# Filler matmuls of an attention stage held at their step, and up to seven of them from the fourth step on

## The chip, the cores and the metric

One core of one Trainium2 chip runs the whole kernel. The metric is device time in microseconds (us), the median of the runs of one kernel on one chip; lower is better. The engines are named as in the profile: PE (matmuls; PEld its weight loads), DVE, ACT, POOL, and SP, which issues the DMAs.

## The reference, cut to what matters

Three parts follow each other on tensors of 4 batches, 576 tokens and 512 columns, all float32.

```
scores = q @ k.T / 8                      # 4 batches, 8 heads, 576 x 576, head size 64
scores = where(scores >= max(scores) - tau, scores, -1e9)
x = softmax(scores) @ v                   # heads joined: 4 x 576 x 512
u = x + (x.T @ U @ V).T                   # mix over the tokens, rank 32
x = u + relu(u @ w_ch1) @ w_ch2           # 512 -> 2048 -> 512
e = routed expert of each token           # 8 experts, by w_gate and a local gate
out = p[e] * (relu(x @ w1[e]) @ w2[e])    # 512 -> 1024 -> 512
```

## The kernel before, in words

Batch 0's attention runs alone (`attention_alone`, line 546): this is the first stage. After it, the attention of batch b runs interleaved with the dense layers (`channel`) of batch b-1, and the experts come last.

The first stage takes 4 pairs of heads, each in 5 row groups of 128 rows. A group has two tiles (the two heads, h = 0 and 1), the last of a pair one: 36 tiles. The name s0_1_3 is the scores of batch 0, pair 1, group 3. One step of the loop handles one tile and touches its neighbours:

- `mask` of the tile before (line 370, DVE), which is the last reader of that tile's scores;
- `scores` of the next tile (lines 320 and 322, PE: four matmuls, eight in group 4). The scores have two PSUM buffers (tag s), so scores of tile i+2 wait for the mask of tile i;
- `peak` (line 355, DVE, the row maximum), `exp` (line 366, ACT) and `limits` (line 359, DVE) of the tile;
- pieces of `back` of earlier groups: transposes of the probabilities (tp, line 423, PE) which ACT copies out (ptt, line 424), products with v (po, lines 442 to 446, PE), and the chain that adds the token mix (lines 468 to 515);
- last, `turn_over` (line 586): filler matmuls on a constant bf16 tile (idle, line 592), whose results nobody reads. Their number is what an estimate of the step's `back` work (`spent`) leaves of 0.8, in units of 0.2, so at most four (four more in step 0, and eight ahead of the loop).

The result tile of a step's fillers is taken in turn from the two PSUM buffers of the transposes (tag tp). So fillers wait for the ACT copy of the transposes that were in that buffer, and a transpose after them for the buffer after that.

A scheduler orders the instructions of each engine before the launch, by what it reckons to be ready; on the chip each engine takes them strictly in that order. `keep_in_program_order` ties an instruction behind the one written before it on its engine. It adds no wait. In the kernel before it holds the first filler of steps 0, 1 and 2 alone. The scheduler may put later fillers earlier, into steps of others.

Into the same stage fall the loads of q and k (raw, line 283; split into kh, kl and qs, lines 291 to 301), and the conversion of the dense weights (`convert`): loaded (cr, line 203), joined on ACT and DVE (lines 211 and 218), written to DRAM (wdram, line 242), and read back as wr (line 681), from which ACT makes w0h and w1h (line 688).

Of the kernel before, what the change touches and what calls it, by code (L numbers as in the profile page):

```python
# [103 lines left out]
def attention_channel_moe(ctx, tc, qk, vv, tau, umat, vrep, wch, wgl, wexp, consts, out):  # L104
# [43 lines left out]
    def bank(tag, shape, name):  # L148
        return BANKS["pool"].tile(shape, F32, tag=tag, name=name, bufs=BANKS["bufs"][tag])
# [370 lines left out]
    def link():  # L520

        while CHAIN:
            try:
                return next(CHAIN[0])
            except StopIteration:
                CHAIN.pop(0)
        return 0.0
# [32 lines left out]
    def attention_alone(b):  # L560

        pend, debt, loads = [], 0.0, []
        inps = {0: load_pair(b, 0)}
        seq = [(hp, g, h) for hp in range(NPAIR) for g in range(5) for h in range(1 if g == 4 else 2)]
        groups = {}

        def scores_of(i):
            hp, g, h = seq[i]
            if h == 0:
                groups[hp, g] = Group(b, hp, g, inps[hp])  # L570
            groups[hp, g].scores(h)

        def tile_of(i):
            if not 0 <= i < len(seq):
                return None, 0
            hp, g, h = seq[i]
            return groups[hp, g], h

        def piece():
            while pend:  # L580
                try:
                    return next(pend[0]) + link()
                except StopIteration:
                    pend.pop(0)
            return link()

        def turn_over(n, nm):

            if n > 0:
                t = bank("tp", [128, 512], f"idle{nm}")  # L590
                for j in range(n):
                    x = pe.matmul(t, lhsT=idle[:, :128], rhs=idle, start=True, stop=True)
                    if j == 0 and nm in (0, 1, 2):
                        tc.keep_in_program_order(x)

        turn_over(8, "a")
        scores_of(0)
        for i in range(len(seq) + 3):
            G, h = tile_of(i)
            P, ph = tile_of(i - 1)  # L600
            Q, qh = tile_of(i - 2)

            if P:
                P.mask(ph)
            if i + 1 < len(seq):
                scores_of(i + 1)
            if G:
                G.peak(h)
                G.exp(h)
                G.limits(h, h + 1)  # L610
            if G and h == 0 and G.key[2] == 1 and G.key[1] + 1 < NPAIR:
                inps[G.key[1] + 1] = load_pair(b, G.key[1] + 1, loads)
            if loads and next(loads[0], 1):
                loads.pop()
            if Q and Q.nh == 1:
                Q.norm()
            debt = max(debt + RATE, 0.0) if pend else 0.0
            spent = piece()
            debt -= spent
            while pend and debt > 0:  # L620
                c = piece()
                debt -= c
                spent += c
            turn_over(int((0.8 - spent) / 0.2) + (4 if i == 0 else 0), i)
            if Q and qh == Q.nh - 1:
                pend.append(back(*Q.key, Q.inp, Q))
            yield i
        while pend or CHAIN:
            piece()
# [236 lines left out]
    with tc.manual_schedule(engines={mybir.EngineType.Pool}):  # L866
        for i in attention_alone(0):
            if i >= 4:
                debt += 0.2 if i > 9 else 1
                while debt > 0:  # L870
                    next(conv, None)
                    debt -= 1
# [514 lines left out]
```

## Time and profile before

| | us |
|---|---|
| median of 3 runs | 1026.74 |
| the runs | 1026.74, 1026.70, 1029.19 |
| the profiled execution, whole | 1029.15 |
| its span | 1027.4 |
| PE busy | 993.8 |
| DVE busy | 718.8 |
| ACT busy | 610.8 |

All rows of the trace are from the one profiled execution; times in them count from the start of its span. A busy engine is one that has an instruction in flight: back-to-back matmuls overlap, so their durations do not add up to the time of a group. The granted clock is the share of TensorE's 2.4 GHz that the chip gave; 0.50 is 1.2 GHz.

### The profile page before, as it was taken

How to read it: one execution, taken by the hardware profiler on the slowest of the kernel's cores; microseconds unless marked ns; L12 is line 12 of the kernel's file. 1: busy time of each engine (PE TensorE's matmuls, PEld its weight loads, DVE VectorE, ACT ScalarE, POOL GpSimd, SP SyncE). 2: the span in 40 equal slices, each digit the busy share in tenths (PEclk: the TensorE clock that was granted, in tenths of full speed). 3: DMA queues.
4: the chain of work that ended last, by engine and by line, in shares of the span. 5: the costliest groups of instructions: out<-in, count | busy, mean ns of one | idle time of the engine just before them, and what ended most of it. 6: DMA issues, size and time to landing. Idle time of an engine off the chain costs nothing. (4 is left out here: it accounts for less than half of the span.)

```text
span 1027.4 us, 17797 instructions
## 1 busy us (share of the span) xinstructions
PE 993.8 (97%) x6309; PEld 831.8 (81%) x6309; DVE 718.8 (70%) x1771; ACT 610.8 (59%) x1242; POOL 157.9 (15%) x149
## 2 busy tenths in 40 slices
PE   8898899999999999999999999999999999999996
PEld 4666677778787787788888898999998798889884
DVE  7889787886778877877676564692469755566673
ACT  6787877776687777776565653432344344355562
POOL 3322145342000000000000000014400321120100
PEclk9999999999999999999999999999999999999998
DMA  7745487864323322423121110463154655566650
GB/s 216 240 126 168 144 265 241 281 204 150 114 97 92 123 80 77 125 95 89 56 68 42 42 45 28 140 212 127 39 196 151 201 178 185 174 193 198 194 184 16
DMA packets 58529, 143.72 MB, mean 140 GB/s; under 512 B 7421, under 2 KB 8573, under 8 KB 58432
## 3 DMA queue, kind: packets, MB, share of 16 engines
q1 hardware_dynamic: 55072, 132.27, 40.2%
q0 software_dynamic: 3360, 10.23, 3.0%
q8 instruction: 52, 0.85, 0.3%
q14 instruction: 45, 0.37, 0.1%
HBM read 124.65 MB, written 18.61 MB: 139 GB/s over the span
## 5 line engine op out<-in xcount | busy, mean ns | idle before, releaser
L1137 ACT ACTIVATE eh<-ew 128x512 fp32r<-128x512 f32 x160 | 94.0, 628 | 66.9 <-PE el L1253 51.8
L1138 DVE TENSOR_TENSOR el<-ew,eh 128x512 fp32r<-128x512 f32 x160 | 106.6, 692 | 37.4 <-ACT eh L1137 34.8
L370 DVE SCALAR_TENSOR_TENSOR p<-s,st,p 128x576 f32<-128x576 f32 x144 | 114.1, 814 | 18.5 <-ACT p L366 14.8
L710 PE MATMUL l<-uh,w0h 128*128 128x256 f32 (+2 forms) x352 | 126.7, 360 | 0.3 <-ACT yT L515 0.3
L366 ACT ACTIVATE p<-s,st 128x576 f32<-128x576 f32 x144 | 103.6, 739 | 34.9 <-DVE st L355 33.7
L711 PE MATMUL l<-ul,w0h 128*128 128x256 f32 (+2 forms) x352 | 122.6, 349 | 0.0
L712 PE MATMUL l<-uh,w0l 128*128 128x256 f32 (+2 forms) x352 | 122.3, 348 | 0.0
L355 DVE TENSOR_REDUCE st<-s 128x1 f32<-128x576 f32 x144 | 105.2, 749 | 16.2 <-PE s L322 15.2
L725 PE MATMUL l<-hh,w1h 128*128 128x512 f32 (+3 forms) x320 | 115.3, 360 | 0.0
L727 PE MATMUL l<-hh,w1l 128*128 128x512 f32 (+3 forms) x320 | 112.6, 352 | 0.0
L726 PE MATMUL l<-hl,w1h 128*128 128x512 f32 (+3 forms) x320 | 112.2, 351 | 0.0
L424 ACT ACTIVATE ptt<-tp 128x512 f32<-128x512 f32 (+1 forms) x192 | 88.6, 490 | 30.7 <-PE tp L423 30.5
L320 PE MATMUL s<-kh,qs 128*128 128x288 f32 x320 | 96.7, 321 | 7.1 <-DVE p L370 4.9
L689 POOL TENSOR_TENSOR w1l<-wr,w1h 128x512 fp32r<-128x512 f32 x24 | 32.4, 1359 | 457.9 <-DVE rha L995 426.2
L423 PE MATMUL tp<-cst,p 128*128 128x128 f32 x576 | 91.2, 276 | 2.6 <-ACT ptt L424 2.2
L730 DVE TENSOR_TENSOR yT<-l,yT 128x448 f32<-128x448 f32 (+2 forms) x96 | 50.0, 521 | 57.7 <-PE l L727 57.3
L322 PE MATMUL s<-kl,qs 128*128 128x288 f32 x320 | 89.6, 299 | 0.0
L380 ACT ACTIVATE p<-p,rv 128x576 f32<-128x576 f32 x108 | 78.6, 771 | 15.7 <-DVE rv L387 15.5
L423 PEld LDWEIGHTS tp<-cst,p 128*128 128x128 f32 x576 | 67.9, 140 | 19.2 <-ACT ptt L424 9.3
L320 PEld LDWEIGHTS s<-kh,qs 128*128 128x128 f32 x320 | 60.9, 190 | 17.1 <-DVE p L370 7.7
L443 PE MATMUL po<-ptt,v 128*64 128x256 f32 (+1 forms) x256 | 71.4, 416 | 2.2 <-ACT ptt L424 2.2
L442 PE MATMUL po<-ptt,v 128*64 128x256 f32 (+1 forms) x256 | 70.8, 416 | 1.3 <-ACT ptt L431 1.0
(610 smaller groups left out, 2441.1 us busy)
## 6 DMA issues: line engine op xcount, KB each, us to landing
ew<-in_wexp_dram SPq DMA_DIRECT2D x80, 512.0 KB, 4.5
wr<-wdram SPq DMA_DIRECT2D x128, 256.0 KB, 2.7
cr<-in_wch_dram SPq DMA_DIRECT2D x32, 512.0 KB, 5.4
raw<-in_qk_dram SPq DMA_DIRECT2D x30, 304.0 KB, 3.5
wdram<-w SPq DMA_DIRECT2D x32, 256.0 KB, 2.9
v<-in_vv_dram SPq DMA_DIRECT2D x16, 352.0 KB, 3.6
raw<-in_qk_dram SPq DMA_DIRECT2D x16, 320.0 KB, 3.1
raw<-in_qk_dram SPq DMA_DIRECT2D x16, 288.0 KB, 4.0
```

What stands on the lines that cost most here:

```text
L320: pe.matmul(s["t"][:, h, :288], lhsT=qs[:, qc:qc + 128], rhs=kh[:, k0:k0 + 288], start=(j == 0), stop=False)
L355: dve.tensor_reduce(out=self.st[:, 0, h:h + 1], in_=self.t[h], axis=AX.XY, op=ALU.max, negate=True)
L366: act.activation(self.halves(h), self.t[h], AF.Exp, bias=self.st[:, 0, h:h + 1])
L370: dve.scalar_tensor_tensor(out=p, in0=self.t[h], scalar=self.st[:, 1, h:h + 1], in1=p, op0=ALU.is_ge, op1=ALU.mult, accum_out=self.rvs[:, ...
L423: pe.transpose(tp[:, c - c0], src[:, c * 128:c * 128 + 128], ident)
L710: pe.matmul(pm, lhsT=w1h[:, wk], rhs=uh[k], start=(k == 0), stop=False)
L711: pe.matmul(pm, lhsT=w1h[:, wk], rhs=ul[k], start=False, stop=False)
L712: pe.matmul(pm, lhsT=w1l[:, wk], rhs=uh[k], start=False, stop=(k == 3))
L725: pe.matmul(pm, lhsT=w2h[:, wd], rhs=xh, start=(f == f0), stop=False)
L726: pe.matmul(pm, lhsT=w2h[:, wd], rhs=xl, start=False, stop=False)
L727: pe.matmul(pm, lhsT=w2l[:, wd], rhs=xh, start=False, stop=(f == f0 + 3))
L1138: dve.tensor_tensor(out=lo, in0=x, in1=hi.bitcast(F32), op=ALU.subtract)
```

## The change

```
         def turn_over(n, nm):
...
                     x = pe.matmul(t, lhsT=idle[:, :128], rhs=idle, start=True, stop=True)
-                    if j == 0 and nm in (0, 1, 2):
+                    if j == 0 and nm != "a":
                         tc.keep_in_program_order(x)
...
-            turn_over(int((0.8 - spent) / 0.2) + (4 if i == 0 else 0), i)
+            turn_over(int(((1.5 if i > 3 else 0.8) - spent) / 0.2) + (4 if i == 0 else 0), i)
```

The first filler of every step is tied behind the instruction written before it on PE. From step 4 on the number is what `spent` leaves of 1.5, at most seven. The program has 78 fillers in place of 35: 8, 8, 4, 4 and 4 ahead of step 4 in both, and then 50 in place of 7 (4 of step 5, and one each of steps 9, 18 and 27).

The scheduler's order of the other instructions in the first stage changes with it, on PE, DVE, ACT and SP; on POOL, and on all engines from some 30 instructions after the start of the dense layers on, it is the same. Three places follow.

PE, steps 3 to 5, before: tp0_0_0_0, _4 and _8 are the transposes of pair 0, group 0 in three buffers' turns, s0_0_2_1 and s0_0_3_0 the scores of group 2, h = 1, and of group 3, h = 0.

```order
L423 MATMUL tp0_0_0_0_247<-cst_62,p0_0_0_150 128x128 x4
L320 MATMUL s0_0_2_1_234<-kh0_98,qs0_97 128x288
L322 MATMUL s0_0_2_1_234<-kl0_99,qs0_97 128x288
L320 MATMUL s0_0_2_1_234<-kh0_98,qs0_97 128x288
L322 MATMUL s0_0_2_1_234<-kl0_99,qs0_97 128x288
L423 MATMUL tp0_0_0_4_253<-cst_62,p0_0_0_150 128x128 x4
L423 MATMUL tp0_0_0_8_259<-cst_62,p0_0_0_150 128x128
L320 MATMUL s0_0_3_0_267<-kh0_98,qs0_97 128x288
L322 MATMUL s0_0_3_0_267<-kl0_99,qs0_97 128x288
L320 MATMUL s0_0_3_0_267<-kh0_98,qs0_97 128x288
L322 MATMUL s0_0_3_0_267<-kl0_99,qs0_97 128x288
```

PE, the same place, after (the scores s0_0_2_1 now stand ahead of the first row):

```order
L423 MATMUL tp0_0_0_0_247<-cst_62,p0_0_0_150 128x128 x4
L423 MATMUL tp0_0_0_4_253<-cst_62,p0_0_0_150 128x128 x4
L423 MATMUL tp0_0_0_8_259<-cst_62,p0_0_0_150 128x128
L320 MATMUL s0_0_3_0_270<-kh0_98,qs0_97 128x288
L322 MATMUL s0_0_3_0_270<-kl0_99,qs0_97 128x288
L320 MATMUL s0_0_3_0_270<-kh0_98,qs0_97 128x288
L592 LDWEIGHTS idle_85
L592 MATMUL idle4_262<-idle_85 128x512
L592 LDWEIGHTS idle_85
L592 MATMUL idle4_262<-idle_85 128x512
L322 MATMUL s0_0_3_0_270<-kl0_99,qs0_97 128x288
```

The transposes moved behind the scores of group 2, and two fillers came between the third and the last matmul of s0_0_3_0; seven of step 5 follow.

ACT, the same steps, before: ptt is the copy of the transposes, p the exp, qs1 the load of pair 1's q out of raw1.

```order
L291 ACTIVATE kh1_202<-raw1_1_224 128x640
L424 ACTIVATE ptt0_0_0_246<-tp0_0_0_0_247 128x4x128
L366 ACTIVATE p0_0_2_214<-s0_0_2_0_216,st0_0_2_215 128x576
L299 ACTIVATE qs1_201<-raw1_2_242,t8_63 128x608
L424 ACTIVATE ptt0_0_0_246<-tp0_0_0_4_253 128x4x128
```

ACT, the same place, after:

```order
L291 ACTIVATE kh1_202<-raw1_1_224 128x640
L366 ACTIVATE p0_0_2_214<-s0_0_2_0_216,st0_0_2_215 128x576
L299 ACTIVATE qs1_201<-raw1_2_242,t8_63 128x608
L424 ACTIVATE ptt0_0_0_246<-tp0_0_0_0_247 128x4x128
L424 ACTIVATE ptt0_0_0_246<-tp0_0_0_4_253 128x4x128
```

The first copy moved behind qs1, which waits for a DMA.

ACT, pair 1, group 3, before: w0h is the first dense weight read back, yT the token mix of pair 0, p0_1_3 the two exps of group 3.

```order
L424 ACTIVATE ptt0_1_0_526<-tp0_1_1_0_594 128x4x128
L515 ACTIVATE yT0_363<-pu0_0_4_0_573 128x256
L688 ACTIVATE w0h0_0_1362<-wr0_0_0_1360 128x512
L515 ACTIVATE yT0_363<-pu0_0_4_256_578 128x320
L366 ACTIVATE p0_1_3_556<-s0_1_3_0_558,st0_1_3_557 128x576
L424 ACTIVATE ptt0_1_0_526<-tp0_1_1_4_600 128x4x128
L424 ACTIVATE ptt0_1_0_526<-tp0_1_1_8_606 128x128
L211 ACTIVATE top0_87<-cr0_1_512_443 128x512
L366 ACTIVATE p0_1_3_556<-s0_1_3_1_585,st0_1_3_557 128x576
```

ACT, the same place, after:

```order
L688 ACTIVATE w0h0_0_1422<-wr0_0_0_1420 128x512
L515 ACTIVATE yT0_371<-pu0_0_4_0_591 128x256
L366 ACTIVATE p0_1_3_574<-s0_1_3_0_576,st0_1_3_575 128x576
L515 ACTIVATE yT0_371<-pu0_0_4_256_596 128x320
L366 ACTIVATE p0_1_3_574<-s0_1_3_1_606,st0_1_3_575 128x576
L424 ACTIVATE ptt0_1_0_544<-tp0_1_1_0_615 128x4x128
L424 ACTIVATE ptt0_1_0_544<-tp0_1_1_4_621 128x4x128
L424 ACTIVATE ptt0_1_0_544<-tp0_1_1_8_627 128x128
```

The second exp moved ahead of all three copies; w0h, which waits for a DMA, still stands ahead of both exps.

## Rows read from the trace of the kernel before

**Rows 1.** Windows by stage: length, busy us of each engine (instructions), clock, DMA share, GB/s.

```profile
core 0: us, PE busy (x) PEld busy (x) DVE busy (x) ACT busy (x) POOL busy (x), PEclk, DMA share, GB/s
...
16.00:44.00 28.00, 24.52 (x171) 17.71 (x170) 26.88 (x66) 23.46 (x50) 9.31 (x8) 1.00 0.75 247
44.00:56.00 12.00, 10.15 (x59) 7.12 (x58) 8.46 (x21) 7.75 (x16) 5.46 (x4) 0.86 0.47 146
56.00:112.00 56.00, 48.74 (x368) 35.56 (x367) 50.24 (x122) 46.91 (x106) 10.30 (x8) 1.00 0.54 157
112.00:990.00 878.00, 870.04 (x5547) 743.39 (x5546) 605.47 (x1502) 509.76 (x1024) 121.60 (x112) 1.00 0.43 138
```

**Rows 2.** Windows of the weak stretch, columns as in Rows 1.

```profile
47.00:48.00 1.00, 0.00 (x0) 0.00 (x0) 0.03 (x1) 1.00 (x4) 0.87 (x1) 1.00 0.86 295
...
49.00:50.00 1.00, 1.00 (x6) 0.62 (x3) 0.05 (x1) 1.00 (x3) 0.00 (x0) 0.50 0.74 234
```

**Rows 3.** Waits of DVE from 16 to 112 us: total us, times, longest.

```profile
DVE p L370 <- ACT p L366: 3.3, 6, 1.0
DVE st L355 <- PE s L322: 2.6, 5, 0.9
DVE xsd L472 <- PE tx L468: 0.8, 2, 0.5
```

**Rows 4.** Timeline of PE: start, us, instruction, count; eight fillers in a row.

```profile
13.68 1.90 PE L592 MATMUL idle<-idle 128*128 128x512 bf16 x8
```

**Rows 5.** Timeline of PE, steps 4 and 5; idle us and releaser in brackets.

```profile
17.17 0.86 PE L423 MATMUL tp<-cst,p 128*128 128x128 f32 x5
19.24 0.40 PE L320 MATMUL s<-kh,qs 128*128 128x288 f32 x1 [1.20 <-DVE p L370]
19.48 0.30 PE L322 MATMUL s<-kl,qs 128*128 128x288 f32 x1
19.61 0.29 PE L320 MATMUL s<-kh,qs 128*128 128x288 f32 x1
```

**Rows 6.** Timeline of ACT, the same steps.

```profile
17.07 0.58 ACT L424 ACTIVATE ptt<-tp 128x512 f32<-128x512 f32 x1
...
18.74 0.80 ACT L299 ACTIVATE qs<-raw,t 128x608 fp32r<-128x608 f32 x1 [0.46 <-DMA raw<-in_qk_dram]
19.45 0.74 ACT L424 ACTIVATE ptt<-tp 128x512 f32<-128x512 f32 x2
```

**Rows 7.** Timeline of DVE, the same steps.

```profile
20.46 0.76 DVE L355 TENSOR_REDUCE st<-s 128x1 f32<-128x576 f32 x1
21.25 0.82 DVE L370 SCALAR_TENSOR_TENSOR p<-s,st,p 128x576 f32<-128x576 f32 x1
```

**Rows 8.** Timeline of ACT around the first dense weight.

```profile
46.43 0.63 ACT L688 ACTIVATE w0h<-wr 128x512 fp32r<-128x512 f32 x1 [0.84 <-DMA wr<-wdram]
...
47.28 0.73 ACT L366 ACTIVATE p<-s,st 128x576 f32<-128x576 f32 x1
47.90 0.76 ACT L424 ACTIVATE ptt<-tp 128x512 f32<-128x512 f32 x2
...
49.17 0.74 ACT L366 ACTIVATE p<-s,st 128x576 f32<-128x576 f32 x1
```

**Rows 9.** Timeline of PE, the same place.

```profile
48.55 0.46 PE L443 MATMUL po<-ptt,v 128*64 128x256 f32 x1 [1.85 <-ACT ptt L424]
```

**Rows 10.** Timeline of DVE, the same place.

```profile
48.05 0.82 DVE L370 SCALAR_TENSOR_TENSOR p<-s,st,p 128x576 f32<-128x576 f32 x1 [1.01 <-ACT p L366]
...
49.95 0.82 DVE L370 SCALAR_TENSOR_TENSOR p<-s,st,p 128x576 f32<-128x576 f32 x1 [0.95 <-ACT p L366]
...
51.71 0.76 DVE L355 TENSOR_REDUCE st<-s 128x1 f32<-128x576 f32 x1 [0.94 <-PE s L322]
```

**Rows 11.** Timeline of SP's DMA queue: the reads of the first dense weights.

```profile
41.03 0.90 SPq L681 DMA_DIRECT2D wr<-wdram  x2
```

**Rows 12.** Window of the transposes (tile tp) alone: PE, PEld, ACT, clock, DMA.

```profile
80.00:82.00 2.00, 0.79 (x8) 0.55 (x6) 0.62 (x2) 1.00 0.62 225
```

**Rows 13.** Timeline of PE: the first matmul of the dense layers.

```profile
114.42 0.50 PE L710 MATMUL l<-uh,w0h 128*128 128x512 f32 x1 [0.32 <-ACT yT L515]
```

More of the change, by code (lines that the diff above doesn't have):

```diff
@@ L592, in turn_over @@
                     x = pe.matmul(t, lhsT=idle[:, :128], rhs=idle, start=True, stop=True)
-                    if j == 0 and nm in (0, 1, 2):
+                    if j == 0 and nm != "a":
                         tc.keep_in_program_order(x)
@@ L623, in attention_alone @@
                 spent += c
-            turn_over(int((0.8 - spent) / 0.2) + (4 if i == 0 else 0), i)
+            turn_over(int(((1.5 if i > 3 else 0.8) - spent) / 0.2) + (4 if i == 0 else 0), i)
             if Q and qh == Q.nh - 1:
```

## The prediction

> **What bounds the kernel now.** I read the windows by stage first [rows 1]. From 112 to 990 us PE is busy for 870.04 of 878 us, at full clock: whatever the first stage gains or loses is passed on one to one, and a matmul that moves out of the long stretch into a gap of the first stage saves its own time. The change touches the first stage only, so everything is decided between 16 and 112 us. There PE is busy for 24.52 + 10.15 + 48.74 = 83.4 us of 96, idle for 12.6. DVE is the denser engine by far in what it has to do: 26.88 of 28 us up to 44, and 50.24 of 56 behind 56. So the stage is set by DVE and by what DVE waits for. These waits come next [rows 3]: masks wait 3.3 us for exps of ACT, peaks 2.6 us for scores of PE, and 0.8 us goes to the token mix. Only the last two, 3.4 us, name PE.
>
> Third, the weak stretch, 44 to 56 us, where DVE is busy for 8.46 of 12 us and the mean granted clock is 0.86 [rows 1]. The order of events: ACT stands for 0.84 us until the first dense weight has landed, and its next exp starts at 47.28 [rows 8]. PE has nothing for 1.85 us, until 48.55 [rows 9]. In 49 to 50 its clock is 0.50, 1.2 GHz [rows 2]. DVE loses 1.01 and 0.95 us on late exps and 0.94 us on late scores, 2.90 us together [rows 10]. This is the only fall of the clock between 16 and 112 us.
>
> **The change part by part.** *More fillers.* Eight in a row take 1.90 us at full clock [rows 4]; the last takes its full 0.38 us to end, so one costs (1.90 - 0.38) / 7 = 0.217 us. There are 43 more, 9.3 us of PE. Beside the 12.6 us that PE is idle this fits in the sum, with 3 us to spare; it does not show that each falls where PE is idle. The cover, worked out: when a mask frees a score buffer, DVE has a peak (0.76 us) and a mask (0.82 us [rows 7]) to do before it wants the next scores, 1.58 us. The four score matmuls start 0.13 us apart and the last takes 0.3 us to end [rows 5], 0.7 us. The remaining 0.88 us hold four fillers. So up to four are free if they start no later than the mask ends, and they cost their time where they start late. Groups of seven exist only in step 5, and there the next scores wait for a mask anyway.
>
> *Steps 4 and 5.* Here I can follow the new order with the old durations. The scores s0_0_3_0 start at 19.24 now, released by a mask, and their peak runs at 20.46 [rows 5, 7]. In the new order the ninth transpose ahead of them reuses the buffer of tp0_0_0_0, whose copy now stands behind qs1. That load starts at 18.74, when its DMA lands, so the copy runs at 19.45 (now it ran at 17.07) and ends at about 20.0 [rows 6]. Transpose and three score matmuls: 20.1 to 20.5. Then two fillers, which wait for the second copy (to 20.4): 20.5 to 20.95. The last score matmul ends at about 21.35. The peak is late by 21.35 - 20.46 = 0.9 us, on DVE, with nothing else queued that could run. PE meanwhile idles from about 18.1 to 20.0. The next scores wait for the mask behind this peak, so the seven fillers of step 5 are hidden. Cost 0.9 us; bounds 0.4 (if only the copy counts) and 1.4 (if the clock falls after that gap too, as it did after 1.85 us [rows 9], at half speed for the fillers and the scores).
>
> *The weak stretch.* No filler stands where the gap is: in the new order PE still waits for the mask of s0_1_3, that for the exp, that for w0h, and that for the DMA. SP issues the read at 41.03 [rows 11]; in the new order it stands behind the same kinds of loads, so I leave it there. The first exp stays at 47.28. What changes is behind it: the second exp comes right after one yT copy, at about 48.25 instead of 49.17 [rows 8], so its mask can follow the first at 48.9 instead of 49.95 and that wait of 0.95 us goes. The scores s0_1_4 get their buffer at 48.9; their second half stands behind a transpose that waits for the copy of tp0_1_1_0 (now behind both exps, to 49.5), two products and four matmuls: they end at 50.6 at full clock, 51.2 at half clock, against 51.71 for the peak now [rows 10]. Gain 0.5 to 1.1 us. I take 0.8.
>
> Here a rule of the Trainium skill bears on what the fillers are for. Rows first: between 56 and 112 us the clock is 1.00 throughout [rows 1], also in 80 to 82, where eight transposes keep PE busy for 0.79 of 2 us [rows 12]. The Trainium skill, "TensorE: Matmul & The Clock Gate", Part 4 (PE-mode transpose), says that transposes do not count as activity for the clock. By that rule a stage with so many transposes needs fillers, and the change would be worth more than I give it. The trace does not bear it out, so I leave it out of the sum.
>
> *The end of the stage.* The new order puts the first four matmuls of s1_0_2 ahead of the dense layers. Now these start at 114.42 after waiting for the last token mix on ACT [rows 13], and those four come later, in the stretch that PE bounds. That moves 4 x 0.13 = 0.5 us into a gap. It is lost again if PE reaches the dense layers late because of them, so the bounds are -0.5 and +0.3.
>
> *The rest.* Some 30 steps keep their work and get other neighbours on DVE and ACT. The masks come earlier against the peaks. With the waits outside the two places at 3.4 + 3.3 - 2.9 = 3.8 us at most, I bound this at -2 (half goes) and +2.5 (half as much again, and the fillers of five steps start one filler late), and take 0.
>
> Sum on the profiled execution: 1029.15 + 0.9 - 0.8 - 0.5 = 1028.75, so -0.4. That execution is one of two kinds: the runs are 1026.70, 1026.74 and 1029.19, and it lies with the slow one. If the fall of the clock is what tells them apart (the 0.94 us and what follows it), the median has less to gain. Against the median, 1026.74 - 0.4: **1026.4 us**.
>
> **The rivals.** *Faster: the stage is freed of PE's delays.* If the fillers keep PE ahead at every step, the 2.90 us of the weak stretch and the other 2.6 - 0.94 = 1.7 us of late scores go: 4.6 us, less what the median run does not have, 1022.2 to 1024; I take 1023.0. For it: the new order alternates peak and mask more evenly, and frees buffers sooner. Against it: only 3.4 us of the waits name PE, the weak stretch is begun by a DMA, and a filler never makes real work earlier.
>
> *Slower: pinned fillers block the scores.* Fillers take a transpose buffer, so each group waits for an ACT copy, and the scores written behind now wait with it on PE. Some ten groups of step 4 and later stand directly ahead of scores or inside a group of them (steps 4, 9, 10, 16, 18, 24, 25, 27, 28, 30). The price of one is the 0.9 us worked out for step 4; if half of them pay it, 4.5 us: 1031.2. It decides where the copy ends later than a mask plus 0.88 us less the fillers' own time, which for four fillers is: later than the mask. For it: ACT is busy for 46.91 of 56 us [rows 1] and its copies stand behind exps. Against it: an exp that delays the copy delays the mask as well.
>
> *The change does not do what it says.* The gap at 47 to 48 lies in a chain of waits, not at the place of a filler; the clock falls there as before, and in the new gap at 18 to 20 perhaps too. Then the time is 1026.4 to 1028.9, still no difference by the bound below.
>
> **How the numbers follow.** A measurement of this kernel tells a change of about 0.3%, 3.1 us, from none. The forecast, with the case that the clock still falls, has 0.58: within 1023.7 and 1029.8. Faster by more has 0.22, slower by more 0.20: the slow rival needs five of ten places, the fast one nearly all of the waits that it names. If all terms go one way their bounds add to 0.4 - 1.1 - 0.5 - 2 = -3.2 and to 1.4 - 0.5 + 0.3 + 2.5 = 3.7; the range reaches a little into both rivals: 1022.8 to 1030.4.
>
> **What would show it.** DVE should wait for about 0.9 us for the scores near 20 us that it does not wait for now, and PE idle for some 2 us ahead of it. The first exp after w0h should start at 47 to 48.5, and the second about 1 us behind it. 78 fillers, with the waits of PE on ptt copies in their rows; the three kinds of DVE's waits [rows 3] at 5 to 9 us together, against 6.7 now. The dense layers should start at 113 to 116. I am wrong if that start moves by more than 3 us, or if the long stretch behind it changes its length.

## The result: 1040.04 us, slower by 1.1%

The changed kernel takes 1040.04 us (median of 4 runs, 1037.62 to 1040.68) against 1027.24 us before (4 runs, 1026.70 to 1029.19). The ratio is 1.011, with a 95% interval of 1.0092 to 1.0128. I had forecast 1026.4 and no difference. The profiled execution took 1040.34 us, 11.2 us more than that of before (1029.15).

The windows by stage, columns as in [rows 1], now read:

```profile
core 0: us, PE busy (x) PEld busy (x) DVE busy (x) ACT busy (x) POOL busy (x), PEclk, DMA share, GB/s
16.00:44.00 28.00, 25.20 (x153) 17.25 (x157) 26.00 (x64) 21.58 (x42) 9.28 (x8) 1.00 0.71 226
44.00:56.00 12.00, 11.24 (x89) 8.22 (x88) 9.08 (x24) 10.47 (x23) 4.67 (x4) 1.00 0.53 170
56.00:112.00 56.00, 49.43 (x348) 36.12 (x353) 45.09 (x107) 43.44 (x94) 11.49 (x9) 1.00 0.48 140
112.00:990.00 878.00, 865.91 (x5531) 739.03 (x5531) 602.08 (x1502) 508.60 (x1024) 120.84 (x112) 1.00 0.41 136
```

The granted clock between 44 and 56 us is 1.00 where it was 0.86. But DVE, the denser engine of the stage, does less in the 56 us behind it: 45.09 us of work for 50.24. PE does hardly more (49.43 for 48.74), although it has fillers to do. So the fillers mostly did not fill idle time; real work moved out of the window. What DVE and PE wait for from 16 to 112 us (total us, times, longest; DVE's rows answer to [rows 3]):

```profile
DVE st L355 <- PE s L322: 9.4, 13, 1.2
DVE p L370 <- ACT p L366: 3.7, 6, 1.0
```

```profile
PE idle L592 <- ACT ptt L424: 2.9, 6, 1.1
PE tp L423 <- ACT ptt L424: 2.0, 5, 0.7
PE pu L514 <- DVE th L501: 1.9, 3, 1.2
PE tT L490 <- ACT xsd L482: 1.4, 2, 0.9
PE s L320 <- DVE st L359: 0.8, 1, 0.8
PE s L320 <- DVE p L370: 0.6, 2, 0.3
```

Peaks wait for scores of PE for 9.4 us where it was 2.6. PE in turn waits for ACT and DVE, and hardly for masks (0.6 us, before 4.3). PE has become the late one. The dense layers, [rows 13] before, start 7.43 us later:

```profile
121.85 0.50 PE L710 MATMUL l<-uh,w0h 128*128 128x512 f32 x1 [0.51 <-ACT yT L515]
```

Behind that start the shift still grows: the last matmul of line 710, near the end of the dense layers, starts at 756.3 us for 742.7, 13.6 us late. The experts behind it give 2.4 us back. One gap stands out near 136 us (timelines of PE, ACT and SP's queue, and the window behind it):

```profile
136.54 0.65 PE L443 MATMUL po<-ptt,v 128*64 128x256 f32 x2 [2.15 <-ACT ptt L424]
```

```profile
133.77 0.78 ACT L211 ACTIVATE top<-cr 128x512 f16<-128x512 bf16 x1 [2.16 <-DMA cr<-in_wch_dram]
```

```profile
127.65 1.79 SPq L203 DMA_DIRECT2D cr<-in_wch_dram  x1
```

```profile
136.00:142.00 6.00, 5.46 (x18) 4.08 (x19) 2.01 (x3) 1.55 (x4) 3.93 (x5) 0.72 0.67 239
```

ACT stands for 2.16 us for a load of the conversion of the dense weights, with the copy that PE needs behind it. PE is idle for 2.15 us, and the mean granted clock from 136 to 142 us is 0.72. In the kernel before the same issue of SP took 0.43 us, ACT stood for its load for 0.73 us, and PE for the copy for 0.32:

```profile
120.22 0.43 SPq L203 DMA_DIRECT2D cr<-in_wch_dram  x1
```

```profile
124.97 0.79 ACT L211 ACTIVATE top<-cr 128x512 f16<-128x512 bf16 x1 [0.73 <-DMA cr<-in_wch_dram]
```

```profile
127.74 0.65 PE L443 MATMUL po<-ptt,v 128*64 128x256 f32 x2 [0.32 <-ACT ptt L424]
```

### The profile page after: what moved, and what is told of

It is laid out like the page before. It is cut to its first block, busy times and chain, and to the rows that moved or that the text cites. A ratio compares the mean times of both kernels' runs of the same rounds, so it can differ in the third digit from the quotient of the medians.

```text
span 1038.6 us, 17859 instructions
## 1 busy us (share of the span) xinstructions
PE 1002.1 (96%) x6343; PEld 837.5 (81%) x6352; DVE 717.7 (69%) x1771; ACT 613.8 (59%) x1242; POOL 157.9 (15%) x149
## 5 line engine op out<-in xcount | busy, mean ns | idle before, releaser
L443 PE MATMUL po<-ptt,v 128*64 128x256 f32 (+1 forms) x256 | 71.3, 414 | 2.1 <-ACT ptt L424 2.1
L714 DVE SCALAR_TENSOR_TENSOR hl<-l,hh 128x512 fp32r<-128x512 f32 (+2 forms) x80 | 46.3, 579 | 38.6 <-ACT hh L713 38.3
```

## The experiments

The table has the ratio to the kernel before (on the same chip, in the same minutes), its 95% interval, and the start of the dense layers in the one profiled execution; before it is 114.42. The absolute times of a kernel differ from chip to chip (the kernel before had medians of 1028.15 to 1033.77 us), so ratios are compared, and starts as one execution each. Runs 1 to 4, 5 to 8, 9 to 11, 12 to 15, 16 and 17, and 18 shared a chip and its runs of before.

| run | order of the real work | fillers of step 4 and later | ratio | interval | dense start, us |
|---|---|---|---|---|---|
| changed kernel | new | 50 | 1.011 | 1.0092 to 1.0128 | 121.85 |
| 1 bare | new | 34, short | 1.0125 | 1.0090 to 1.0161 | 121.42 |
| 2 half | new | 50, half length | 1.0110 | 1.0081 to 1.0139 | 121.49 |
| 3 pin only | old but for 4 places | 7 | 0.9993 | 0.9977 to 1.0008 | 112.90 |
| 4 more only | between | 50 | 1.0087 | 1.0069 to 1.0105 | 121.32 |
| 5 old order | old | 50 | 1.0043 | 1.0020 to 1.0066 | 119.77 |
| 6 new order | new | 7 | 1.0072 | 1.0035 to 1.0109 | 123.69 |
| 7 first half | new to 68 us | 7 | 1.0057 | 1.0031 to 1.0083 | 118.48 |
| 8 second half | new from 68 us | 7 | 1.0087 | 1.0057 to 1.0118 | 118.74 |
| 9 old order, bare | old | 36, short | 1.0048 | 1.0030 to 1.0067 | 116.30 |
| 10 scores first | scores early | 50 | 1.0147 | 1.0113 to 1.0180 | 131.81 |
| 11 same, before | scores early | 7 | 1.0029 | 1.0014 to 1.0045 | 117.82 |
| 12 no turn | old | 50, no own bank | 1.0064 | 1.0045 to 1.0083 | 118.90 |
| 13 run 5 again | old | 50 | 1.0070 | 1.0057 to 1.0083 | 118.32 |
| 14 run 6 again | new | 7 | 1.0069 | 1.0057 to 1.0081 | 119.67 |
| 15 changed again | new | 50 | 1.0101 | 1.0086 to 1.0116 | 124.86 |
| 16 scores whole | new, 13 tiles mended | 50 | 1.0111 | 1.0080 to 1.0142 | 122.52 |
| 17 same, before | old, 9 tiles mended | 7 | 1.0019 | 1.0001 to 1.0036 | 118.38 |
| 18 spared | old | 38 | 1.0039 | 1.0023 to 1.0056 | 116.31 |

The starts carry less than the ratios. Two executions of one program differ in theirs by 1.5 us (runs 5 and 13), 3.0 (the changed kernel and run 15) and 4.0 (runs 6 and 14). The profiled executions of runs 13 and 14 took 2.4 and 2.5 us less than the median of their run, that of run 8 7.5 us less, that of run 17 4.0 us more.

A second table shows where time is lost: by how much the peak (line 355) of the last tile of each pair of heads starts later than in the profile of before, from DVE's timelines, then the dense layers and the last matmul of line 710, near their end. In runs 5 and 13 one record of a peak is missing; their later peaks are counted accordingly. Run 8 has the order of before up to the middle of pair 2. It and run 3 show that the execution of before had itself lost over a microsecond by the end of pair 1.

| | pair 0 | pair 1 | pair 2 | pair 3 | dense layers | last of line 710 |
|---|---|---|---|---|---|---|
| start before, us | 25.99 | 51.71 | 74.47 | 95.76 | 114.42 | 742.7 |
| 3 pin only | +0.66 | -1.23 | -1.47 | -1.52 | -1.52 | -0.4 |
| 8 second half | +0.52 | -1.35 | +1.93 | +4.07 | +4.32 | +5.2 |
| changed kernel | +0.91 | +0.94 | +3.52 | +7.24 | +7.43 | +13.6 |
| 15 changed again | +1.02 | +0.95 | +5.54 | +9.20 | +10.44 | +13.2 |
| 14 new order | +0.65 | +0.05 | +2.39 | +5.01 | +5.25 | +6.4 |
| 6 new order | +1.52 | +0.99 | +3.15 | +7.19 | +9.27 | +11.5 |
| 13 old order, 50 fillers | +1.05 | +0.13 | +2.22 | +3.36 | +3.90 | +6.6 |
| 5 old order, 50 fillers | +1.90 | +0.38 | +2.47 | +3.61 | +5.35 | +7.9 |
| 9 old order, short fillers | +0.57 | -0.12 | +0.51 | +0.47 | +1.88 | +4.0 |
| 18 spared | +1.44 | +0.07 | +0.88 | +1.29 | +1.89 | +5.9 |
| 16 scores whole | +1.24 | +1.11 | +4.41 | +7.71 | +8.10 | +13.6 |

**Which half of the change costs?** Runs 3 and 4 make one half each (edits against the changed kernel).

```
-            turn_over(int(((1.5 if i > 3 else 0.8) - spent) / 0.2) + (4 if i == 0 else 0), i)
+            turn_over(int((0.8 - spent) / 0.2) + (4 if i == 0 else 0), i)
```

> Only the first half of the change: the first filler of every step is held at its step, the number stays at what is left of 0.8 (35 fillers). The order of the real work differs from before in four places only, all near steps 4 and 5. Both theories: no difference, 1026 to 1029, the dense layers at 114 to 115. If holding alone costs, as my slow rival has it, up to 0.9 us for each of the held groups of step 4 and later.

```
-                    if j == 0 and nm != "a":
+                    if j == 0 and nm in (0, 1, 2):
```

> Only the second half: 78 fillers, held in steps 0 to 2 alone, so the scheduler may put the others earlier, where it takes PE to be idle; its order of the real work lies between before and after. Theory A: the same 10.8 us of PE; if they float into idle time they are free, 1027 to 1030, if not, as the changed kernel, 1036 to 1041. Theory B: as far as the order is that of the changed kernel, the same loss; the order differs in about half of the rows, so 1030 to 1040.

Holding alone, with 7 late fillers, is free: 0.9993. The number alone costs 0.87%, most of the whole. So the holding, on which my slow rival rested, is not needed for the loss; whether it adds something to 50 fillers is open, since the intervals of run 4 and of the changed kernel overlap. Run 3 also has the clock at 1.00 in the weak stretch, with no filler there:

```profile
44.00:56.00 12.00, 10.31 (x68) 7.21 (x65) 9.99 (x27) 10.08 (x23) 5.45 (x4) 1.00 0.58 172
```

The order is not what keeps it up either. Run 8 (below) follows the kernel before in this stretch and has 1.00 too. ACT does not stand for the dense weight there, and PE's gap is 0.90 us in place of 1.85 (window, ACT, PE, and the two peaks at the ends of the stretch):

```profile
44.00:56.00 12.00, 10.31 (x67) 7.11 (x65) 10.01 (x27) 10.09 (x23) 5.46 (x4) 1.00 0.57 173
```

```profile
46.09 0.62 ACT L688 ACTIVATE w0h<-wr 128x512 fp32r<-128x512 f32 x1
```

```profile
48.21 0.43 PE L443 MATMUL po<-ptt,v 128*64 128x256 f32 x1 [0.90 <-ACT ptt L424]
```

```profile
46.89 0.75 DVE L355 TENSOR_REDUCE st<-s 128x1 f32<-128x576 f32 x1
...
51.89 0.76 DVE L355 TENSOR_REDUCE st<-s 128x1 f32<-128x576 f32 x1 [0.19 <-PE s L322]
```

The same two peaks before, and in the changed kernel:

```profile
46.28 0.75 DVE L355 TENSOR_REDUCE st<-s 128x1 f32<-128x576 f32 x1
...
53.86 0.73 DVE L355 TENSOR_REDUCE st<-s 128x1 f32<-128x576 f32 x1
```

```profile
48.47 0.76 DVE L355 TENSOR_REDUCE st<-s 128x1 f32<-128x576 f32 x1
...
54.96 0.75 DVE L355 TENSOR_REDUCE st<-s 128x1 f32<-128x576 f32 x1
```

The stretch takes 7.58 us before, 5.00 in run 8 and 6.49 in the changed kernel. Of the three profiles with the order of before in this stretch (before, runs 3 and 8), only that of before has the wait for the weight and the fall of the clock.

**Is it the fillers' own time?** In runs 1 and 2 the program is built as the changed kernel, and the filler instructions are then altered in place, so that nothing else moves. In run 1 those that carry a wait or a signal are cut to 32 columns and the others taken out; in run 2 all of step 4 and later are cut to 256.

```
+    drop(nc, lambda i: i > 3, 32)
```

> Every instruction stands in the order of the changed kernel; in the built program 16 of the 50 fillers of step 4 and later are taken out and the other 34, which carry a wait or a signal, are cut from 512 columns to 32. Theory A (the fillers' own PE time stands ahead of the scores): 50 x 0.217 = 10.8 us of PE go, of which 34 short ones keep perhaps 2; the waits of DVE for scores fall from 9.5 us to about 3, the dense layers start at 114 to 116 us in place of 121.85, and the time is 1027 to 1032. Theory B (the changed order of the real work, with the waits on the two transpose buffers, costs the time): the waits for scores stay at 8 to 10 us, the dense layers start at 120 to 122, the time is 1037 to 1041. If the clock falls again near 47 us for want of fillers, 1 to 2 us more in either. If the second loss (4 us between 122 and 240 us) comes with the order at the boundary, it stays under A too: 1031 to 1036.

```
+    shorten(nc, lambda i: i > 3, 256)
```

> The order of the changed kernel; the 50 fillers of step 4 and later are cut from 512 to 256 columns in the built program. Theory A (fillers' time): they take half, 5.4 us of 10.8; the dense layers start at 117 to 119 us, halfway between 114.4 and 121.85. Theory B (order and buffer waits): 120 to 122, and 1037 to 1041 in all.

Theory A, that the fillers' own time costs, is out as the main cause in the changed kernel: with nearly all of that time gone, the dense layers start only 0.43 us earlier and the ratio is 1.0125. Between the ends of pairs 1 and 3 run 1 still loses 5.2 us, where the changed kernel loses 6.3. The late scores stay (DVE's waits in run 1, 16 to 112 us):

```profile
DVE st L355 <- PE s L322: 8.3, 13, 1.1
DVE p L370 <- ACT p L366: 3.1, 4, 0.9
```

What the fillers do is to change the order: the scheduler reckons with their time when it draws up the order of everything else.

**The order and the fillers apart.** Edges that add no wait put the instructions of PE, DVE, ACT and SP of one kernel into the order of the other. (With its own order put in by such edges, the kernel before comes out instruction for instruction, so the edges cost nothing.) Run 5 has the fillers' number and the old order; run 6 the new order and the old number.

```
+        for a, b in zip(order, order[1:]):
+            tc.add_manual_dep(own[b], own[a].name, mybir.DependencyInfo(
+                mybir.DependencyClass.NoSync, mybir.DependencyReason.DATA), reason="follow")
```

> 78 full fillers, at nearly the places that they have in the changed kernel (7 behind the second score of step 5's tile, groups of 1 to 4 after), but every other instruction of PE, DVE, ACT and SP in the order of the kernel before; that order is imposed by edges that add no wait. Theory B (the scheduler's new order of the real work costs the time, the fillers' 0.217 us each are free): the dense layers start at 113 to 116 us, the time is 1026 to 1030. Theory A' (the fillers cost time by standing ahead of scores, whatever the order): 120 to 122 us and 1036 to 1041. The clock between 44 and 56 us should be 1.00 if the fillers keep it up.

> The kernel before, with its 35 fillers, and every other instruction of PE, DVE, ACT and SP in the order of the changed kernel. So none of the 50 later fillers is there, and none of their waits for an ACT copy of transposes. Theory B (order): the dense layers start at 120 to 122 us, the time is 1035 to 1041. The rival within it, that the fillers' waits for the transposes' buffers cost the time (my slow rival; the run with short fillers kept those waits): 114 to 117 us, 1027 to 1032.

Both cost. Runs 13 to 15 put these two and the changed kernel on one chip:

> The run with 78 fillers in the old order once more, beside the other three on one chip, for the share of the fillers' waits and turns. If order and waits add up to the whole: 1.003 to 1.006 here, 1.005 to 1.008 for the new order, 1.009 to 1.012 for the changed kernel. If either alone is enough: 1.008 to 1.012 in all three.

> The run with the new order and the 35 fillers of before once more, on the same chip. If order and waits add up: 1.005 to 1.008. If the order alone makes the whole loss: as the changed kernel, 1.009 to 1.012.

> The changed kernel itself, on the same chip and with a second profile. Ratio 1.009 to 1.013. If the gap of PE near 134 to 137 us and the fall of the clock behind it belong to this order, they are in this profile too, and the shift grows from 7 us at the dense start to 11 or more at 240 us; if they were chance, the shift stays at 7 to 10 us.

The new order alone costs 0.69%, the fillers alone 0.70%, both together 1.01%. Either alone makes two thirds of the loss, and they do not add up. I had expected them either to add up or to be enough alone; it is neither. (The same two programs on another chip gave 0.72% for the order, run 6, and 0.43% for the fillers, run 5.) In the new order alone peaks wait 7.5 us for scores (run 14; run 6 10.0), nearly as in the changed kernel; before it was 2.6:

```profile
DVE st L355 <- PE s L322: 7.5, 11, 1.1
```

So the order is enough for the late scores. What the fillers add to it, 0.3% between runs 14 and 15, does not go with their length in run 1, whose interval starts at 1.0090 (on another chip). Whether it is their waits for the two banks was not tested in the new order. Run 15 also settles that the gap near 136 us belongs to the changed kernel, since it is there again, 3 us later with the rest. The fall of the clock behind it is not there again (1.00 from 139 to 145 us):

```profile
139.56 0.65 PE L443 MATMUL po<-ptt,v 128*64 128x256 f32 x2 [2.16 <-ACT ptt L424]
```

In run 14, with the same order but the stage 5 us earlier, the wait there is 0.86 us:

```profile
133.07 0.65 PE L443 MATMUL po<-ptt,v 128*64 128x256 f32 x2 [0.86 <-ACT ptt L424]
```

**Which stretch of the order?** Runs 7 and 8 change over from one order to the other in the middle of pair 2.

```
+FOLLOW = {e: new[e][:cut[e]] + old[e][cut[e]:] for e in new}
```

> The kernel before with the changed kernel's order up to the middle of the third pair of heads (about 68 us: PE as far as the second scores of group 2) and its own order from there on. If the late scores are spread evenly, about half of the 7.4 us: the dense layers start at 117 to 119 us. If the loss is made where the first pair's steps 4 and 5 are, 119 to 122. The second loss behind the first stage (4 to 6 us) stays away if it comes from the order at the boundary: 1029 to 1032 in all; it is there if it comes from being late: 1032 to 1036.

> The reverse: the order of the kernel before up to the middle of the third pair, the changed kernel's from there on. Evenly spread late scores: the dense layers start at 117 to 119 us. If the second loss comes from the order at the boundary it is here: 1033 to 1038 in all; if not, 1029 to 1032.

The start moves by 4.1 and 4.3 us, near half each, as an even spread has it; with an execution of run 8 so far below its median this is a hint only. The ratios say no more than that each costs: 1.0057 and 1.0087 have intervals that overlap, and the second loss could not be read from them.

**Why do the fillers cost in the old order?** Three runs keep the old order. Run 9 cuts the fillers short as in run 1. In run 12 they take no bank of their own but are written into the tile of the next transposes, so that the waits and turns of the two banks go.

```
+    drop(nc, lambda i: i > 3, 32)
```

> The run with 78 fillers in the old order, whose dense layers started at 119.8 us, but in the built program 14 of the 50 later fillers are taken out and the other 36, which carry a wait or a signal, are cut to 32 columns. If in the old order the fillers cost by their own time, the start returns to 114 to 116 us and the time to that of before. If they cost by their waits for the transposes' buffers, and by the turn that they take of the two buffers, the start stays at 118 to 120 us.

```
                 tp = bank("tp", [128, 4, 128], f"tp{nm}_{c0}")
+                for _ in range(min(DUE[0], 4)):
+                    x = pe.matmul(tp.rearrange("p a b -> p (a b)"), lhsT=idle[:, :128], rhs=idle, start=True, stop=True)
```

> 78 full fillers and the order of the kernel before for all other work, as in the run with the old order, but the 50 later fillers take no bank of their own: they are written into the tile of the next transposes, just ahead of these, so they add no wait for an ACT copy that the transposes don't have anyway and no turn of the two banks. If the fillers' waits and turns cost the 0.4 to 0.5% that the old order with fillers showed, the time is that of before, ratio 0.998 to 1.002, the dense layers at 113 to 116 us. If the fillers' own 10.8 us of PE cost it, the ratio is 1.003 to 1.007 and the start 117 to 121 us.

Run 12 is against my rival: without own waits and turns the cost is still 0.64%. Run 9 is for the fillers' time inside the stage: the last peaks of its pairs follow those of before to within 0.6 us up to 96 us, where run 13 loses 3.4. So here, other than in the new order, the length of the fillers matters. A reason shows in windows of 8 us. The kernel before:

```profile
64.00:72.00 8.00, 7.84 (x66) 5.94 (x65) 6.71 (x20) 6.50 (x15) 1.27 (x1) 1.00 0.47 152
72.00:80.00 8.00, 7.95 (x59) 6.14 (x59) 7.44 (x20) 7.43 (x15) 2.93 (x2) 1.00 0.59 151
...
88.00:96.00 8.00, 7.59 (x71) 6.47 (x71) 6.57 (x18) 6.88 (x18) 1.92 (x3) 1.00 0.43 124
```

PE was already busy for 15.79 of the 16 us from 64 to 80. The 7.26 us that it was idle between 56 and 112 lie elsewhere. Run 18 leaves out the 12 fillers that fell into these stretches:

```
-            if n > 0:
+            if n > 0 and nm not in (21, 23, 24, 25, 30, 32):
```

> The run with 78 fillers in the old order, less the 12 fillers of steps 21, 23, 24, 25, 30 and 32, which fell into 67 to 78 and 89 to 94 us; 66 fillers stay. In the kernel before PE was busy for 15.8 of the 16 us from 64 to 80 and for 7.6 of 8 from 88 to 96, and less elsewhere. If the fillers cost where PE has no idle time of its own, the loss goes with these 12: dense layers at 113 to 116 us in place of 118.3 and 119.8, ratio 0.999 to 1.003. If they cost everywhere, 12 of 50 go: 117 to 119 us, ratio 1.003 to 1.006. If any foreign instruction in this order costs the same (the short fillers showed 1.0048), the ratio stays at 1.004 to 1.007.

Between the ends of pairs 1 and 3 the peaks lose 1.2 us in place of 3.2, and the dense layers start at 116.31 in place of 118.32 and 119.77. That is for the local lack of idle time, as to the stage; the start lies just above the 113 to 116 that I gave. The total is less clear: 1.0039 lies where I put a cost everywhere, and its interval (1.0023 to 1.0056) overlaps that of run 5, though not that of run 13. Run 9 has the same split: a start only 1.9 us late, and 1.0048. So some of the loss of these two arises behind the first stage: by the last matmul of line 710 they are 5.9 and 4.0 us late. None of the runs shows by what.

**Is it how the scores stand among other work?** Run 10 gives the scores of the first stage the scheduler's highest priority in the changed kernel, run 11 in the kernel before.

```
-            groups[hp, g].scores(h)
+            with tc.high_priority(): groups[hp, g].scores(h)
```

> The changed kernel with the scores of the first stage given the scheduler's highest priority, so that they stand ahead of transposes, products and the token mix as soon as their buffer is reckoned free; 78 fillers, nearly all at full length and in other places. If peaks that wait for scores behind other work of PE are what costs, DVE's waits for scores fall from 9.4 us to 3 or less and the dense layers start at 113 to 117 us; 1027 to 1032 in all. If the stage is late for another reason (ACT, or the token mix that is now pushed back), the waits move there and the start stays at 119 to 123 us.

> The kernel before with the scores given the highest priority. If late scores are what is left to gain, 2.6 us of waits go at most: the dense layers start at 111.5 to 114 us, the time is 0 to 3 us below before. If it only makes PE wait for masks with transposes and products standing behind, the start is 115 to 119 us and the time 1 to 5 us above before.

Both are slower, run 10 by most of all. The products that were pushed back are then late for ACT, 6.3 us at one place (waits of ACT, 16 to 112 us):

```profile
ACT yT L449 <- PE po L446: 8.4, 3, 6.3
```

Next, a piece of the changed kernel's timelines, PE and then DVE. It shows the scores of pair 2, group 3 around the token mix of pair 1:

```profile
70.00 0.38 PE L320 MATMUL s<-kh,qs 128*128 128x288 f32 x1
71.31 0.42 PE L490 MATMUL tT<-xsd,u_sb 128*32 128x128 f32 x8 [0.93 <-ACT xsd L482]
71.55 0.24 PE L492 MATMUL tT<-xsd,u_sb 128*32 128x32 f32 x8
71.73 0.40 PE L322 MATMUL s<-kl,qs 128*128 128x288 f32 x1
```

```profile
72.43 0.76 DVE L355 TENSOR_REDUCE st<-s 128x1 f32<-128x576 f32 x1 [0.71 <-PE s L322]
```

The first of four score matmuls runs at 70.00, then the token mix stands for ACT, and the other three come 1.7 us late; the peak waits. Run 16 puts the four side by side in the 13 tiles that are split so, run 17 in the 9 of the kernel before. One place in PE's order, each name with its count of matmuls, in the changed kernel and in run 16:

```
-s0_2_3_0*1 tT0_1_4*8 s0_2_3_0*3 tp0_2_0_8*1 s0_2_3_1*2 rep0_1_4*1 pu0_1_4_0*2 s0_2_3_1*2
+s0_2_3_0*4 tT0_1_4*8 tp0_2_0_8*1 s0_2_3_1*4 rep0_1_4*1 pu0_1_4_0*3
```

> The changed kernel (78 fillers) in its own order, but with the four matmuls of a tile's scores put side by side in the 13 tiles where transposes, products or parts of the token mix stand among them, which in the trace make PE wait for ACT or DVE with two or three score matmuls behind. If this splitting is what costs, most of the 6 to 8 us that the peaks lose between 59 and 96 us comes back: dense layers at 115 to 118 us, ratio 1.002 to 1.006. If it is the places of the whole blocks ahead of the scores, the gain is small: 120 to 124 us, ratio 1.008 to 1.012.

> The kernel before with the same edit in its 9 such tiles. If splitting costs there too, up to 1 to 2 us of the late scores go: ratio 0.998 to 1.000, dense layers at 112 to 114 us. If the split was the better order there (the rest of the scores was to wait for nothing that PE could not do meanwhile), the token mix comes later and the ratio is 1.000 to 1.004.

It changes nothing: 1.0111, and 122.52 us. The trace of run 16 shows why. The scores stand together from 70.18 on, and the token mix behind them stands still, now with the next tile's scores behind it:

```profile
70.18 0.38 PE L320 MATMUL s<-kh,qs 128*128 128x288 f32 x1
...
72.50 0.42 PE L490 MATMUL tT<-xsd,u_sb 128*32 128x128 f32 x8 [1.55 <-ACT xsd L482]
...
73.07 0.38 PE L320 MATMUL s<-kh,qs 128*128 128x288 f32 x1
```

So here it is the place of the token mix against what feeds it, not the split. In the old order five transposes stand between these scores and tT, and two more behind it, so that PE has work while ACT and DVE do their part of the chain; in the new order nothing does. The kernel before, where PE does not wait at tT:

```profile
68.50 0.98 PE L423 MATMUL tp<-cst,p 128*128 128x128 f32 x5
69.42 0.43 PE L490 MATMUL tT<-xsd,u_sb 128*32 128x128 f32 x8
```

That this holds for all of the places is not shown; no run moved the token mix alone.

None of these kernels beats the kernel before; run 3 is the same.

## Why the prediction was wrong, step by step

- **"43 more fillers, 9.3 us, fit in the sum".** This is the first step that failed. The 12.6 us of idle PE were a sum over 96 us. From 64 to 80 us PE had 0.21 us to spare, and six steps put 12 fillers there and into 88 to 96. I wrote that the sum "does not show that each falls where PE is idle" and did not look at shorter windows, though the trace had them. The price is shown in the old order: 3.2 us between the ends of pairs 1 and 3 (runs 5 and 13), 0.6 with short fillers (run 9), 1.2 without those 12 (run 18). In the changed kernel the fillers' length is a small part at most: run 1 loses 5.2 us there with short ones, the changed kernel 6.3 and run 15 8.3.
- **"The rest", taken as 0 with bounds -2 and +2.5.** Mis-sized, and the failure that decides. From the end of pair 1 to that of pair 3 the changed kernel loses 6.3 us (8.3 in run 15). I took it that some thirty steps get other neighbours at no price. The new order alone loses 5.0 us there in run 14 and 6.2 in run 6, and peaks wait 7.5 and 10.0 us for scores of PE.
- **Steps 4 and 5, +0.9 us.** Near in size, by luck. The peak that ran at 20.46 [rows 7] runs at 21.22, 0.76 us later. But the peak two tiles ahead of it was 0.43 us late already (16.77 for 16.34), so this place adds 0.33 (0.62 in run 15). Its wait for scores is 0.20 us, where I had said about 0.9, and PE stands for the copy for 0.55 us, not for 2. Run 3 has the same 0.55 us and loses nothing between the two peaks (3.99 us for 4.12), so the copy behind qs1 alone is no cost. One difference is the two fillers inside the scores: the fourth score matmul starts 0.39 us behind the third in the changed kernel and 0.13 in run 3.
- **The weak stretch, -0.8 us.** The number came out, 1.09 us between the two peaks, but not by the step that I described. The second exp does come 0.94 us behind the first; I had said about 1. The first runs at 48.52, where I left it at 47.28 [rows 8]: all had become later by then. Yet run 8, in the order of before, takes 5.00 us over the same stretch, 1.5 less than the changed kernel. I had read the loss of one execution as a loss of the order. My doubt that the fall of the clock might be what tells the executions apart was the better guess.
- **The end of the stage, -0.5 us.** The gain did not come. From the last peak of batch 0 to the dense layers the changed kernel needs 0.2 us more, run 15 1.2. Within its bound of +0.3 once, once not.
- **"Passed on one to one."** Wrong. I had priced nothing behind 112 us, since the change touched only the first stage; but the loads and conversions behind it were placed in time against it. The shift grows in the dense layers, from 7.4 to 13.6 us in the first profile and from 10.4 to 13.2 in run 15, at the gap near 136 among others, which comes from a load of the conversion. The experts give 2.4 and 2.3 us back, which leaves 11.2 and 10.9. Run 3, the same in time as before, grows there too, by 1.1 us, so not all of it is the change's. What else makes it grow is not shown.
- **The rivals.** The slow one had the right sign and the wrong mechanism and size: the number costs without the holding (run 4), and in the old order fillers without waits of their own cost as much as with them (run 12). PE does stand at fillers for a copy in the changed kernel, for 2.9 us, but for 2.6 in run 14 with its 7 late fillers as well. It gave 4.5 us, the profile has 11.2. That 1026.4 stood on an order read with old durations at three places, and on zero at thirty, is what the range should have shown: its upper end left the unknown rest 2.5 us.
- **The rule on transposes.** The Trainium skill, "TensorE: Matmul & The Clock Gate", Part 4 (PE-mode transpose), says that a transpose does not count as busy PE in the way that other matmuls do. By that rule fillers would have been worth more. No run here needs it: run 3, with 35 fillers, has a granted clock of 1.00 from 16 to 112 us. The stage holds many other matmuls, so this does not test the rule by itself.

## What to carry to other kernels

Before adding work to an engine that "has idle time", read its busy share in windows about as long as a step or two, not over the stage: the idle time may be where the new work won't be. Where a scheduler draws the order from reckoned durations, an instruction that nobody waits for still moves everything else; make it free of time (short, order kept) and compare, which tells its own cost from that of the new order. And before a forecast counts on a loss that one execution shows, see whether another execution of the same order has it.

## What the runs showed of the hardware

The clock fell behind gaps of PE, but not behind each of them. In run 14 PE was busy for 0.41, 0.38 and 0.43 us in the three us from 56 to 59, and the granted clock was 0.50, 1.2 GHz, from 60 to 63 (the first us of the one stretch and the last of the other):

```profile
56.00:57.00 1.00, 0.41 (x4) 0.24 (x3) 0.97 (x3) 1.00 (x3) 0.02 (x1) 1.00 0.74 230
...
62.00:63.00 1.00, 1.00 (x6) 0.75 (x4) 0.59 (x1) 0.57 (x2) 0.00 (x0) 0.50 0.77 165
```

In run 13 it was idle for 1.38 us before 49.70, with 0.31 and 0.30 us of work in the two us from 48 to 50, and the clock stayed at 1.00:

```profile
48.00:49.00 1.00, 0.31 (x2) 0.00 (x0) 0.63 (x1) 1.00 (x3) 0.72 (x1) 1.00 0.18 68
49.00:50.00 1.00, 0.30 (x4) 0.20 (x4) 0.81 (x3) 1.00 (x4) 0.54 (x1) 1.00 1.04 293
```

Two executions of one program can differ in that: run 6 has 0.94 between 16 and 44 us and run 14 has 1.00.

The issue of one load by SP took 1.79 us in the changed kernel and 0.43 before (1.70 in run 15, 0.43 in run 1 with the same order and short fillers). What held it is not shown.
